# A fused S5 and LayerNorm kernel on one core: other queues for the early loads, other PSUM banks for the first transposes, a shorter TensorE warm-up and a new written order

## The chip, the core and the metric

The kernel runs on one core of a Trainium2 chip. The metric is device time in microseconds (us) of one execution. Matmuls run on TensorE (PE, with its weight loads in a row of their own, PEld), elementwise work on VectorE (DVE), ScalarE (ACT) and GpSimd (POOL); SyncE (SP), ACT and POOL issue DMAs from queues of their own. Every engine runs its own instructions strictly in the order in which they were written and waits for the others by semaphores.

## The reference

`x` is one sequence of 2048 tokens with 1024 features, in bf16, as all inputs are. The output is the sum of three terms:

```
xn  = layernorm(x)                                  # over the 1024 features
dt  = exp(log_dt);  L = exp(dt * (Lambda_re + i Lambda_im))
Bu  = xn @ (((L - 1) / Lambda)[:, None] * (B_re + i B_im)).T     # 1024 states, complex
h_t = L * h_{t-1} + Bu_t                            # a scan over the 2048 tokens
A   = 2 * real(h @ (C_re + i C_im).T) + xn * Dskip
r   = xn @ w_r;  the two tokens with the largest r are taken
y   = (silu(xn_sel @ w_gate) * (xn_sel @ w_up)) @ w_down * sigmoid(r_sel)
out = x + A + (xn, with y added to the rows of the two tokens)
```

## The kernel before

Tokens are worked on in 16 chunks of 128 (index c) and 8 frames of 256 (index f); the states in 8 blocks of 128 (index j). For a chunk: x is loaded (`x.c`, L164, L173 or L230); for chunks 0 to 5 DVE takes the statistics in two halves (`bs.c`, `bn.c`, L294 and L297), ACT makes 1/sqrt of the variance from a logarithm and an exponential (`rstd.c`, L262 and L263), DVE applies them (`applyA` and `apply.0` for the halves of chunk 0, L330; `apply.c`, L323), PE transposes the result into a PSUM bank by matmuls with the identity (`TpeA` and `Tpe.0`, L373; `Tpe.c`, L367), and ACT copies it to SBUF as `xnT` (`xnT.c`, L378 and L380; the second half of chunk 0 is copied by DVE, `xnT0`, L383). Chunks 6 to 15 are normalised by ACT and transposed by DMA.

For a frame and a block of states, PE multiplies `xnT` by the transposed B (`Bu.f.j`, L652, 16 matmuls; the first blocks are split by chunk into `Bh.f.j` and `Bu.f.j`), and ACT copies the result out (`u`, L658). For a chunk DVE multiplies by a table (L702, L703), runs the scans (L722), and multiplies back (`TO.c`, L763 to L765) into `hT`. PE then multiplies `hT` by C (`Y.c`, L839), DVE adds the skip term (L850), and the chunk is stored (L854). The carry from chunk to chunk is on POOL. The matmuls of the selected tokens are interleaved later.

The tables need the parameters Lambda_re, Lambda_im, log_dt and w_r. They are loaded as four pieces of 8 rows of one tile `prow` (L169), transposed by one PE instruction (`pP`, L467) and copied by DVE (`pcol`, L470). Then come a product (`angle`, L493 to L501), sines and cosines on ACT (`sin` L517, `first` L512 and L513, `cos` L520), an inverse by logarithm and exponential (`inv`, L530 and L531) and products on DVE (`rc`, L534, and others). ACT loads another function table before the sines (L505) and the first one again behind them (L508). POOL computes small factors (`kappa`, L565 to L571).

The order of all this is the string ORDER, written out by hand: `Plan.emit` calls the functions in exactly that order, and `Plan.run` only asserts that each one stands behind what it depends on and that buffers come free in time. The numbers for durations and keys in the `add` calls don't change the order. Outside ORDER, at the program's start, stand the loads of x.0, x.1, x.2 and of the parameters, ACT's first table load (L176), and the constants. PE starts with a warm-up (`warm.0` to `warm.22`): 23 steps, of which steps 8 to 10 are one matmul of 512 columns (`prime`, L282) and the others two matmuls of 128 columns (L399).

Of the kernel before, what the change touches and what calls it, by code (L numbers as in the profile page):

```python
# [25 lines left out]
B.0.0 xa x.0 x.1 B.0.1 bs.0 bn.0 nmean.0 start.0 x.3 x.2 rstd.0 bs.1 bn.1 applyA apply.0 bs.2 rstd.1 apply.1 nmr1.0 warm.0 warm.1 warm.2 warm.3 warm.4  # L26
warm.5 warm.6 warm.7 warm.8 warm.9 warm.10 warm.11 warm.12 B.1.1 warm.13 warm.14 warm.15 warm.16 warm.17 warm.18 warm.19 warm.20 warm.21 warm.22 TpeA
Tpe.0 xnT0 bn.2 bs.3 bn.3 xnT.0 pP.0 Tpe.1 xnT.1 Bh.0.0 Bu.0.0 B.1.0 B.3.0 nmean.1 nmr1.1 nmean.2 rstd.2 nmr1.2 apply.2 Tpe.2 nmr.2 rstd.3 nmean.3
pcol.0 rsum Bh.0.1 Bu.0.1 nmr.1 u.0.0 wr B.2.0 dt x.5 apply.3 Tpe.3 xnT.2 Bh.1.1 Bh.1.0 B.2.1 frq rad turns whole angle abs trig den x.4 xnT.3 Bu.1.0
Bu.1.1 B.3.1 u.0.1 sin bs.5 bn.5 first Bh.1.2 Bu.1.2 bs.4 x.6 B.4.1 cos u.1.0 u.1.1 Bu.1.3 log bn.4 nmr.3 nmr1.3 sq1.0 rstd.4 apply.4 inv.0 sq1.1 rc.0  # L30
R0.0 Bu.0.2 B.7.0 B.4.0 nmean.5 R.0 Tpe.4 u.1.2 Bu.0.3 rstd.5 apply.5 nmean.4 B.5.0 nmr.5 nmr1.5 u.1.3 Bu.0.4 inv.1 tan.0 u.0.2 Tpe.5 Bu.1.4 rc.1
tan.1 B.5.1 cs ntan.0 nmr1.4 kappa sum.6 R0.1 u.0.3 Bu.1.5 ts.0.0 ts.1.0 B.6.1 TI.0.0 nmean.6 R.1 E2c.0 x.7 u.0.4 B.6.0 B.7.1 C.0.0 cin.0.0 SC.0.0.0
ends xr.0 C.0.1 ntan.1 sq.6 u.1.4 x.8 Bu.0.5 Bu.0.6 u.1.5 xnT.4 u.0.5 Bu.0.7 Bu.1.6 sum.7 xnT.5 u.0.6 nmean.7 sq.7 Bu.1.7 nmr.0 ts.0.1 u.0.7 Bu.2.0
u.1.6 u.1.7 E2c.1 nmr.4 E2n.1 SC.0.0.1 cw.0.0 gb.0.0.0 cy.0.0 cin.1.0 gb.0.0.1 rstd.7 Bu.2.1 ts.1.1 E2s.1 TI.1.0 TI.0.4 TI.1.4 E2n.0 cin.0.4 C.1.0
SC.0.4.0 SC.0.4.1 u.2.0 u.2.1 nmr.7 E2s.0 apply.7 T.7 xr.1 Bu.2.2 Bu.2.3 Bu.2.4 u.2.2 Bu.2.5 gb.0.4.0 cw.0.4 gb.0.4.1 SC.1.0.0 cy.0.4 cin.1.4 nmr1.7
TO.0.0 u.2.3 cw.1.0 SC.1.0.1 cy.1.0 Drow rstd.6 nmr.6 apply.6 T.6 x.9 x.10 u.2.4 SC.1.4.0 cw.1.4 Bu.2.6 Bu.2.7 xnT.6 gb.1.0.1 seed.0.0 TO.0.4 seed.0.1
gb.1.0.0 Y.0.0 gb.1.4.0 u.2.5 u.2.6 SC.1.4.1 xs.0 xr.2 gb.1.4.1 xs.1 cin.2.0 cy.1.4 TI.2.0 TI.3.0 C.1.1 Y.0.1 Y.0.2 u.2.7 TO.1.0 sum.9 nmean.9
seed.1.0 xnT.7 Bu.3.0 Bu.3.1 u.3.0 Bu.3.2 sq.9 rstd.9 nmr1.9 nmr.9 TO.1.4 u.3.1 Y.1.0 Y.1.1 xm.0 cin.2.4 x.12 ADD.0.0 seed.1.1 out.0.0 apply.9 Y.0.3
SC.2.0.0 SC.2.0.1 Bu.3.3 cw.2.0 Bu.3.4 xm.1 T.9 u.3.2 Bu.3.5 ADD.1.0 cy.2.0 TI.4.0 gb.2.0.0 sum.8 out.1.0 ADD.0.1 gb.2.0.1 xs.2 nmean.8 cin.3.0 Y.1.2
Y.1.3 w.0 xm.2 sum.12 seed.2.0 nmean.12 xnT.9 SC.3.0.0 r.0 sq.8 rstd.8 nmr.8 cw.3.0 apply.8 x.11 u.3.3 u.3.4 u.3.5 SC.3.0.1 cy.3.0 cin.4.0 gb.3.0.1  # L40
TO.2.0 T.8 gb.3.0.0 ADD.1.1 out.1.1 SC.4.0.0 SC.4.0.1 out.0.1 cw.4.0 cy.4.0 cin.5.0 sq.12 Bu.3.6 Bu.3.7 rstd.12 xnT.8 Y.2.0 Bu.4.0 nmr.12 xr.3 nmr1.6
sum.11 seed.2.1 nmean.11 TO.3.0 Y.2.1 nmr1.12 ADD.2.0 u.3.6 seed.3.0 u.3.7 Y.2.2 Y.2.3 xs.3 xm.3 apply.12 Bu.4.1 gb.4.0.0 T.12 out.2.0 gb.4.0.1
seed.3.1 Y.3.0 TI.5.0 u.4.0 u.4.1 ADD.2.1 sum.10 SC.5.0.0 cw.5.0 xr.4 Bu.4.2 xs.4 Y.3.1 gb.5.0.0 u.4.2 sq.11 TO.4.0 SC.5.0.1 xr.5 Y.3.2 Y.3.3 seed.4.0
out.2.1 Bu.4.3 Bu.4.4 w.1 cy.5.0 w.2 nmean.10 sq.10 rstd.10 nmr.10 apply.10 T.10 gb.5.0.1 ADD.3.0 ADD.3.1 xnT.10 Y.4.0 Bu.4.5 rstd.11 u.4.3 Y.4.1
seed.4.1 w.3 xm.4 Bu.4.6 cin.6.0 TI.6.0 SC.6.0.0 SC.6.0.1 cw.6.0 nmr.11 ADD.4.0 apply.11 xr.6 Y.4.2 x.14 u.4.4 TO.5.0 u.4.5 gb.6.0.0 u.4.6 gb.6.0.1
nmr1.10 Bu.4.7 T.11 xnT.11 x.13 seed.5.0 seed.5.1 cy.6.0 out.3.1 TI.7.0 Y.4.3 ADD.4.1 w.4 Y.5.0 xs.5 Y.5.1 out.3.0 sum.13 u.4.7 Bu.5.0 Bu.5.1 out.4.0
xm.5 nmean.13 sq.13 xs.6 seed.6.0 cin.7.0 SC.7.0.0 SC.7.0.1 rstd.13 nmr.13 x.15 ADD.5.0 TO.6.0 gb.7.0.0 Y.5.2 Y.5.3 xr.7 Bu.5.2 gb.7.0.1 xm.6 apply.13
seed.6.1 u.5.0 Y.6.0 Y.6.1 sum.14 Bu.5.3 TI.8.0 ADD.5.1 nmean.14 sq.14 out.4.1 rstd.14 nmr.14 w.5 u.5.1 Bu.5.4 Y.6.2 out.5.0 cw.7.0 xr.9 cy.7.0
cin.8.0 SC.8.0.0 SC.8.0.1 TI.9.0 TO.7.0 u.5.2 Bu.5.5 xnT.12 cw.8.0 cy.8.0 cin.9.0 seed.7.0 Y.6.3 T.13 sum.15 xnT.13 nmean.15 sq.15 nmr1.11 ADD.6.0
ADD.6.1 rstd.15 nmr1.15 nmr.15 apply.15 T.15 u.5.3 Bu.5.6 gb.8.0.1 apply.14 xnT.15 gb.8.0.0 SC.9.0.0 SC.9.0.1 TO.8.0 cw.9.0 T.14 xnT.14 Y.7.0 out.5.1  # L50
u.5.4 Bu.5.7 u.5.5 r.1 xs.7 Y.7.1 seed.7.1 xr.8 u.5.6 u.5.7 nmr1.8 rsb seed.8.0 rT cand nmr1.14 Y.7.2 xm.7 ADD.7.0 Y.8.0 xs.8 xm.8 out.6.0 pI cy.9.0
cin.10.0 seed.8.1 idx gather gb.9.0.1 Bu.6.0 u.6.0 Bu.6.1 out.6.1 u.6.1 w.6 out.7.0 gb.9.0.0 TI.10.0 SC.10.0.0 SC.10.0.1 xs.9 TO.9.0 w.7 Bu.6.2 Bu.6.3
u.6.2 Y.8.1 Y.8.2 u.6.3 gb.10.0.0 bns gb.10.0.1 rstds Y.7.3 ADD.7.1 Bu.6.4 ADD.8.0 out.8.0 norm Y.8.3 ADD.8.1 hot Bu.6.5 cw.10.0 xm.9 out.8.1 seed.9.0
sT out.7.1 seed.9.1 xT cy.10.0 Bu.6.6 cin.11.0 mm.0 ymb0 u.6.4 u.6.5 Y.9.0 TI.11.0 Y.9.1 sig SC.11.0.0 SC.11.0.1 xr.10 u.6.6 seed.10.0 gb.11.0.0
ADD.9.0 Y.9.2 seed.10.1 gb.11.0.1 Bu.6.7 u.6.7 w.8 w.9 w.10 Y.9.3 TO.10.0 w.11 out.9.0 mm.1 TI.12.0 cw.11.0 xs.10 xm.10 cy.11.0 Y.10.0 Y.10.1 Y.10.2
exp.0 gu.0 ADD.9.1 ADD.10.0 xr.11 seed.11.0 guT.0 Bu.7.0 u.7.0 nmr1.13 cin.12.0 Y.10.3 w.12 w.13 w.14 w.15 xs.11 w.16 w.17 w.18 SC.12.0.0 gT.0
gb.12.0.0 cw.12.0 SC.12.0.1 sig1 mm.2 exp.1 gb.12.0.1 ADD.10.1 cy.12.0 xr.12 TO.11.0 Bu.7.1 w.19 w.20 w.21 w.22 w.23 Bu.7.2 seed.11.1 seed.12.0 u.7.1
u.7.2 Y.11.0 w.24 w.25 gu.1 guT.1 Y.11.1 xr.13 cin.13.0 out.9.1 Bu.7.3 u.7.3 mm.3 exp.2 TI.13.0 SC.13.0.0 SC.13.0.1 gb.13.0.0 gb.13.0.1 xm.11 ADD.11.0
seed.12.1 Bu.7.4 u.7.4 gT.1 out.10.1 xs.12 w.26 gu.2 Bu.7.5 u.7.5 Bu.7.6 u.7.6 TI.15.0 w.27 w.28 w.29 TO.12.0 Bu.7.7 u.7.7 guT.2 xm.12 gT.2 mm.4
Y.11.2 TO.13.0 out.10.0 w.30 Y.12.0 xs.13 exp.3 TI.15.4 TI.14.0 w.31 Y.12.1 Y.11.3 TI.15.6 ADD.11.1 w.32 w.33 mm.5 gu.3 cw.13.0 cy.13.0 out.11.0  # L60
seed.13.0 ADD.12.0 cin.14.0 SC.14.0.0 seed.13.1 gb.14.0.0 SC.14.0.1 xm.13 Y.12.2 Y.12.3 cw.14.0 cy.14.0 cin.15.0 Y.13.0 w.34 w.35 w.36 ADD.12.1 w.37
gb.14.0.1 w.38 w.39 xr.14 seed.14.0 w.40 w.41 out.11.1 TO.14.0 guT.3 Y.13.1 Y.13.2 Y.13.3 gT.3 ADD.13.0 seed.14.1 SC.15.4.0 SC.15.4.1 ADD.13.1 mm.6
mm.7 Y.14.0 SC.15.0.0 SC.15.0.1 xr.15 rows row_.3 row_.1 row_.2 Y.14.1 Y.14.2 Y.14.3 SC.15.6.0 SC.15.6.1 ymb hotY.14.1 hotY.14.0 xs.14 seed.15.0 xm.14
TO.15.0 ADD.14.0 seed.15.1 ADD.14.1 seed.15.2 out.12.1 TO.15.4 TO.15.6 out.12.0 hotY.15.0 Y.15.0 Y.15.1 Y.15.2 Y.15.3 Y.15.4 Y.15.5 Y.15.6 Y.15.7
hotY.15.2 hotY.15.1 Y.15.8 xs.15 xm.15 ADD.15.0 ADD.15.1 ADD.15.2 out.13.0 out.13.1 fix out.14.0 out.14.1 out.15.0 out.15.1 out.15.2
# [39 lines left out]
def kernel(  # L105
# [135 lines left out]

    add(("xa",), "none", 2.85, lambda: None, key=-1)
    for c in range(NCH):
        if c < 3:
            add(("x", c), "none", (3.35, 0.6, 0.6)[c], lambda: None, [("x", c - 1)] if c else [], key=c, takes=[("xt", c, [("apply", c)])])
        elif c == 3:
            add(("x", c), "SP", 0.45, lambda c=c: load_x(c), key=-89.85, takes=[("xt", c, [("apply", c)])], mb=0.28, lag=0.2)
# [917 lines left out]
```

## Time and profile before

| what | value |
|---|---|
| time, median of 3 runs | 255.83 us (255.74 to 256.82) |
| the profiled execution's own time | 255.56 us |
| its span | 253.8 us |
| PE busy | 246.7 us, 97% of the span, 2052 matmuls |
| DVE busy | 239.8 us, 94%, 312 instructions |
| ACT busy | 175.5 us, 69% |
| POOL busy | 93.1 us, 37% |
| DMA | 46.50 MB, mean 183 GB/s |
| chain that ended last | PE 65%, DVE 25%, POOL 3%, ACT 2%, DMA 1% |

The span runs from the first to the last instruction of the execution; about 1.8 us of the execution's time lie around it. Busy time of two engines overlaps. The chain is followed back from the last instruction to whatever released each step.

### The profile page before, as it was taken

Reading aid. Unit: us, or ns where it says so; the run is one execution under the profiler, and the core shown is the slowest. Engines: PE = TensorE matmul, PEld = TensorE weight load, DVE = VectorE, ACT = ScalarE, POOL = GpSimd, SP = SyncE. Lnnn points to the kernel's source line nnn. Section 1 sums busy time; section 2 is a strip of 40 time slices with the busy share of each in tenths; the row PEclk is TensorE's granted clock in tenths of the full one; section 3 lists DMA queues with packets and bytes.
Section 4 is the critical chain, followed back from the end, with each engine's and each line's share of the span. In section 5 each row is a group of like instructions: output and inputs, shape, how many; then the busy total and the mean of one; then the engine's idle time right before and its main releaser. Section 6 shows DMA issues by size and latency. Waiting matters only on the chain.

```text
span 253.8 us, 5220 instructions
## 1 busy us (share of the span) xinstructions
PE 246.7 (97%) x2052; PEld 167.0 (66%) x2052; DVE 239.8 (94%) x312; ACT 175.5 (69%) x302; POOL 93.1 (37%) x130
## 2 busy tenths in 40 slices
...
GB/s 196 225 228 184 191 254 274 148 134 198 99 159 45 83 89 242 40 256 228 120 89 1 105 166 69 76 3 155 321 340 381 361 316 388 384 250 357 23 68 83
DMA packets 66277, 46.50 MB, mean 183 GB/s; under 512 B 45828, under 2 KB 52362, under 8 KB 66252
## 3 DMA queue, kind: packets, MB, share of 16 engines
...
q8 instruction: 16, 0.26, 0.4%
q0 software_dynamic: 112, 0.27, 0.3%
...
## 4 chain that ended last, share of the span: by engine, by line
PE 65%; DVE 25%; POOL 3%; ACT 2%; DMA 1%; issue 1%; ACTq 0%; DVEq 0%; POOLq 0%
PE pY L839 38%; PE pB L652 22%; DVE gf L722 7%; PE pG L1043 3%; DVE v L703 3%; DVE m L702 2%; DVE m L764 1%; DVE hT L763 1%; DVE ot L850 1%; DVE hT L765 1%; PE pD L1083 1%; DMA xt<-in_A_x_dram 1%; DVE st L294 1%; DVE ts L585 1%; DVE E2c L591 1%
## 5 line engine op out<-in xcount | busy, mean ns | idle before, releaser
L652 PE MATMUL pB<-xnT,BT 128*128 128x256 bf16 (+1 forms) x1104 | 116.9, 265 | 0.6 <-ACT xnT L378 0.3
L839 PE MATMUL pY<-CT,hT 128*128 128x512 bf16 (+1 forms) x528 | 115.7, 373 | 0.2 <-DVE hT L765 0.2
L652 PEld LDWEIGHTS <-BT 128*128 128x128 bf16 x1104 | 100.9, 98 | 16.4 <-issue 1.7
L839 PEld LDWEIGHTS <-hT 128*128 128x128 bf16 x528 | 50.8, 98 | 55.4 <-issue 2.1
L738 POOL TENSOR_TENSOR cw<-gf,tL 128x16 f32<-128x16 f32 (+1 forms) x34 | 41.1, 1210 | 110.8 <-DVE gf L722 101.3
L722 DVE TENSOR_TENSOR_SCAN gf<-R,v 128x1040 f32<-128x1040 f32 (+1 forms) x34 | 68.8, 2056 | 0.5
L658 ACT CAST u<-pB 128x512 bf16<-128x512 f32 x64 | 35.7, 577 | 18.3 <-PE pB L652 15.5
L815 ACT ACTIVATE pY<-xr,nmr_all,rstd_all 128x512 f32<-128x512 bf16 (+1 forms) x33 | 24.9, 763 | 29.2 <-DVE ot L850 24.7
L728 ACT CAST gb<-gf 128x1024 bf16<-128x1024 f32 (+1 forms) x34 | 31.4, 941 | 8.0 <-DVE gf L722 8.0
L850 DVE TENSOR_TENSOR ot<-pY,ot 128x512 bf16<-128x512 f32 (+1 forms) x33 | 21.5, 663 | 3.3 <-PE pY L839 2.1
L765 DVE TENSOR_TENSOR hT<-hT,m 128x2048 bf16<-128x2048 bf16 (+2 forms) x20 | 20.2, 1012 | 0.7
L703 DVE TENSOR_TENSOR v<-u,m 128x2048 bf16<-128x2048 bf16 (+2 forms) x20 | 20.2, 1012 | 0.7
L702 DVE TENSOR_TENSOR m<-u,E1t 128x2048 bf16<-128x2048 bf16 (+2 forms) x20 | 20.1, 1005 | 0.6
L764 DVE TENSOR_TENSOR m<-gb,E2s 128x2048 bf16<-128x2048 bf16 (+2 forms) x20 | 20.3, 1014 | 0.0
L824 ACT ACTIVATE ot<-xr,nmr_all,rstd_all 128x1024 bf16<-128x1024 bf16 x16 | 19.8, 1237 | 0.6 <-DMA out_dram<-ot 0.5
L763 DVE TENSOR_TENSOR hT<-gb,E2c 128x2048 bf16<-128x2048 bf16 (+2 forms) x20 | 20.0, 1000 | 0.0
L753 POOL CAST v<-cy 128x16 bf16<-128x16 f32 (+1 forms) x17 | 12.7, 747 | 1.0
L754 POOL TENSOR_TENSOR v<-cy,v 128x16 bf16<-128x16 f32 (+1 forms) x17 | 12.5, 738 | 1.4
L334 ACT ACTIVATE xn<-xt,nmr_all,rstd_all 128x1024 bf16<-128x1024 bf16 x10 | 12.4, 1237 | 0.2
L309 ACT ACTIVATE xn<-xt,nmean_all 128x1024 bf16<-128x1024 bf16 x10 | 11.5, 1150 | 0.2
L829 DVE TENSOR_TENSOR ot<-ot,Drow 128x1024 bf16<-128x1024 bf16 x16 | 10.9, 680 | 0.0
L303 ACT ACTIVATE xn<-xt 128x1024 bf16<-128x1024 bf16 x10 | 10.5, 1050 | 0.0
...
## 6 DMA issues: line engine op xcount, KB each, us to landing
...
```

Of the source, the lines that this page charges most:

```text
L652: nc.tensor.matmul(out=pB[:, ri, ts_], lhsT=BT[ri][j][:, k, :], rhs=xnT_frame(f)[:, k, ts_], start=(k == 0), stop=(k == DT - 1))
L658: nc.scalar.copy(out=u_tiles[f][:, :, j, :], in_=pB_tiles.pop((f, j))[:])
L702: nc.vector.tensor_tensor(out=m[:, :, js, :], in0=u[:, ::-1], in1=E1t[:, :, js, :], op=ALU.mult)
L703: nc.vector.tensor_add(out=rot, in0=u, in1=m[:, :, js, :])
L722: nc.vector.tensor_tensor_scan(out=flat(gf), data0=flat(R[:, js, :]), data1=flat(v[:, ri, js, :]), initial=0.0, op0=ALU.mult, op1=ALU.add)
L728: nc.scalar.copy(out=gb_tiles[c][:, ri, js, :], in_=gf_tiles[c, js.start, ri][:, :, 2:])
L738: nc.gpsimd.tensor_tensor(out=cw_tiles[c, js.start][:, ri, :, 0:n], in0=g.unsqueeze(1).to_broadcast([128, 2, n]), in1=tL[:, ri, :, js], op ...
L764: nc.vector.tensor_tensor(out=m[:, :, js, :], in0=g[:, ::-1], in1=both(E2s, js), op=ALU.mult)
L765: nc.vector.tensor_add(out=rot, in0=rot, in1=m[:, :, js, :])
L815: nc.scalar.activation(out=pY[:, 0:d_.stop - d_.start], in_=y_tiles["xr", c][:, d_], func=ACT.Identity, bias=nmr_all[:, c:c + 1], scale=rs ...
L839: nc.tensor.matmul(out=pY, lhsT=h_tiles[c][:, ri, j, :], rhs=CT[ri][h][:, j, d0:d0 + w], start=False, stop=end, skip_group_check=True)
L850: nc.vector.tensor_add(out=ot, in0=y_tiles.pop(("pY", c, dh))[:, 0:d_.stop - d_.start], in1=ot)
```

## The change

1. ACT's queue issues four transfers before its table load in place of six: Lambda_re, Lambda_im, log_dt and x.1. The fourth parameter, w_r, is issued by POOL behind its two iotas, and x.2 by SP.
2. SP issues x.3 and x.2 directly behind x.0, and only then the first transposing loads of B (`B.0.0`, `B.0.1`); `x.3` was behind these two.
3. Chunk 0 is transposed into two PSUM banks, one half into the bank with the tag T and the other into that with the tag misc; before, both halves were in T. Chunk 1 uses one of the three banks of the tag B; before, misc.
4. The warm-up has 15 steps in place of 23, that is 16 matmuls of 128 columns fewer.
5. ORDER is rewritten from end to end. On PE, `pP` now stands ahead of chunk 0's transposes, and both `Tpe.3` and `Tpe.2` stand ahead of `Bh.0.1`.

```diff
 ORDER = """
-B.0.0 xa x.0 x.1 B.0.1 bs.0 bn.0 nmean.0 start.0 x.3 x.2 rstd.0 bs.1 bn.1 applyA apply.0 bs.2 rstd.1 apply.1 ...
+x.3 xa bs.0 x.2 warm.0 ... x.0 bn.0 x.1 warm.10 warm.11 bs.1 bn.1 rstd.0 applyA ... pP.0 apply.0 bs.3 pcol.0 apply.1 TpeA Tpe.0 ...
...
-    load_param(nc.scalar, 0)
-    for c in (1, 2):
-        nc.scalar.dma_start(out=xt_tiles[c][:], in_=x2[c * T:(c + 1) * T, :])
-    for i in range(1, 4):
+    for i in range(3):
         load_param(nc.scalar, i)
+    nc.scalar.dma_start(out=xt_tiles[1][:], in_=x2[T:2 * T, :])
     nc.scalar.preload_act_table_set("natural_log_exp_and_others")
...
     nc.vector.tensor_copy(out=tt[:], in_=t_i[:])
+    load_param(nc.gpsimd, 3)
...
-        pT_tiles[c] = psum.tile([128, DT, 128], BF16, name="pT", tag="misc" if odd else "T")
+        pT_tiles[c] = psum.tile([128, DT, 128], BF16, name="pT", tag="B" if c == 1 else "misc" if odd else "T", bufs=3 if c == 1 else 1)
...
     def transpose_half(h):
-        if h == 0:
-            pT_tiles[0] = psum.tile([128, DT, 128], BF16, name="pT", tag="T")
+        pT_tiles[0, h] = psum.tile([128, DT // 2, 128], BF16, name="pT", tag="misc" if h else "T")
...
-    NWARM = 23
+    NWARM = 15
```

The first place is the start of ACT's instructions, up to the first logarithm of `rstd.0`. Before:

```order
L169 DMA prow<-in_A_Lambda_re_dram 8x128
L173 DMA xt<-in_A_x_dram 128x1024 x2
L169 DMA prow<-in_A_Lambda_im_dram 8x128
L169 DMA prow<-in_A_log_dt_dram 8x128
L169 DMA prow<-in_B_w_r_dram 8x128
L176 ACT_TABLE_LOAD
L262 ACTIVATE lv<-mv,eps_t 128x1
```

The same place now:

```order
L169 DMA prow<-in_A_Lambda_re_dram 8x128
L169 DMA prow<-in_A_Lambda_im_dram 8x128
L169 DMA prow<-in_A_log_dt_dram 8x128
L173 DMA xt<-in_A_x_dram 128x1024
L174 ACT_TABLE_LOAD
L261 ACTIVATE lv<-mv,eps_t 128x1
```

The transfer of w_r and that of x.2 are gone from ACT, and x.1 stands behind three parameters in place of one.

The second place is DVE from `applyA` and `apply.0` (the row with x2) on; mv holds a chunk's mean and variance, st its partial statistics. Before:

```order
L330 TENSOR_SCALAR xn<-xt,mv,rstd_all 128x512 x2
L294 BN_STATS st<-xt 128x6
L323 TENSOR_SCALAR xn<-xt,mv,rstd_all 128x1024
L383 COPY xnT<-pT 128x4x128
L294 BN_STATS st<-xt 128x6
L297 BN_AGGR mv<-st 128x2
L294 BN_STATS st<-xt 128x6 x2
L297 BN_AGGR mv<-st 128x2
L323 TENSOR_SCALAR xn<-xt,mv,rstd_all 128x1024
L470 CAST pcol<-pP 128x32
```

The same place now:

```order
L329 TENSOR_SCALAR xn<-xt,mv,rstd_all 128x512 x2
L293 BN_STATS st<-xt 128x6
L468 CAST pcol<-pP 128x32
L322 TENSOR_SCALAR xn<-xt,mv,rstd_all 128x1024
L381 COPY xnT<-pT 128x4x128
L293 BN_STATS st<-xt 128x6
L296 BN_AGGR mv<-st 128x2
L293 BN_STATS st<-xt 128x6 x2
L296 BN_AGGR mv<-st 128x2
L471 CAST wr_cm<-pcol 128x8
L477 TENSOR_TENSOR scr<-scr,pcol 128x8
L478 SCALAR_TENSOR_TENSOR frq<-scr,pcol 128x8
```

The copy of the parameters moves ahead of `apply.1`, and the applies of chunks 3 and 2 come behind the parameters' products.

The third place is ACT around the sines and cosines (sf and cf hold them, th the angle, gf the inverse). Before:

```order
L517 ACTIVATE sf<-th 128x1024
L512 ACTIVATE scr<-th 128x8
L513 ACTIVATE scr<-cf,halfpi 128x8
L520 ACTIVATE cf<-cf,halfpi 128x1024
L658 CAST u<-pB 128x2x256 x2
L508 ACT_TABLE_LOAD
L262 ACTIVATE lv<-mv,eps_t 128x1
L263 ACTIVATE rstd_all<-lv 128x1
L530 ACTIVATE gf<-th 128x4x128
```

The same place now:

```order
L510 ACTIVATE scr<-th 128x8
L511 ACTIVATE scr<-cf,halfpi 128x8
L518 ACTIVATE cf<-cf,halfpi 128x1024
L656 CAST u<-pB 128x2x256
L515 ACTIVATE sf<-th 128x1024
L506 ACT_TABLE_LOAD
L656 CAST u<-pB 128x2x256
L261 ACTIVATE lv<-mv,eps_t 128x1
L262 ACTIVATE rstd_all<-lv 128x1
L528 ACTIVATE gf<-th 128x4x128
```

The sine moves from ahead of the cosine to behind it, and one of the two copies of `u` to behind the table load.

## Rows read from the trace of the kernel before

**Rows 1.** Stretches: us, busy us (count) by engine, clock, DMA share, GB/s.

```profile
1.36:3.04 1.68, 1.68 (x16) 1.68 (x17) 0.96 (x6) 0.00 (x0) 0.61 (x5) 1.00 0.47 139
3.04:4.32 1.28, 1.28 (x5) 0.46 (x4) 0.89 (x2) 0.00 (x0) 0.00 (x0) 1.00 0.98 349
4.32:5.07 0.75, 0.75 (x9) 0.75 (x7) 0.72 (x3) 0.21 (x1) 0.12 (x1) 1.00 1.15 296
5.07:6.02 0.95, 0.95 (x19) 0.94 (x17) 0.94 (x2) 0.95 (x1) 0.13 (x1) 1.00 1.30 279
14.23:78.07 63.84, 63.84 (x579) 51.47 (x576) 61.43 (x90) 56.48 (x106) 27.48 (x46) 1.00 0.88 184
...
83.26:249.40 166.14, 166.14 (x1264) 101.54 (x1265) 160.51 (x183) 106.70 (x175) 56.44 (x60) 1.00 0.58 189
```

**Rows 2.** Chain that ended last, near the middle: start us, us, what.

```profile
81.97 1.24 DVE hT L765
...
83.26 1.90 PE pY L839 x8
```

**Rows 3.** Chain that ended last among the first 12 us.

```profile
1.36 3.17 DMA xt<-in_A_x_dram
...
4.55 0.28 ACTq L169
...
4.86 1.28 ACT L176
...
6.48 0.21 ACT rstd_all L263
```

**Rows 4.** DVE in order of time: start us, us, what [idle before <-releaser].

```profile
4.78 1.23 DVE L294 BATCH_NORM_STATS2 st<-xt 128x6 f32<-128x512 bf16 x2
...
6.71 0.74 DVE L330 TENSOR_SCALAR xn<-xt,mv,rstd_all 128x512 bf16<-128x512 bf16 x2 [0.46 <-ACT rstd_all L263]
...
15.88 0.69 DVE L501 TENSOR_SCALAR cf<-th 128x1024 int32<-128x1024 int32 x1
...
21.40 0.55 DVE L323 TENSOR_SCALAR xn<-xt,mv,rstd_all 128x1024 bf16<-128x1024 bf16 x1 [0.56 <-ACT rstd_all L263]
...
29.48 1.31 DVE L585 TENSOR_TENSOR ts<-sf,scr 128x512 f32<-128x512 f32 x2 [0.46 <-POOL scr L571]
```

**Rows 5.** ACT in order of time.

```profile
2.23 0.36 ACTq L169 DMA_DIRECT2D prow<-in_A_Lambda_im_dram  x1
...
8.87 0.58 ACT L378 COPY xnT<-pT 128x512 bf16<-128x512 bf16 x1 [1.76 <-DVE xnT L383]
...
16.01 1.07 ACT L517 ACTIVATE sf<-th 128x1024 f32<-128x1024 f32 x1
...
22.46 0.57 ACT L658 CAST u<-pB 128x512 bf16<-128x512 f32 x1
```

**Rows 6.** The tiles of x, first 16 us: SP's issues (ns), landing.

```profile
L230 SPq DMA_DIRECT2D xt<-in_A_x_dram x4: 507/519/584, 5.2 to 15.7; - x4
...
DMA to landing us min/median/max: 2.1/3.1/3.5
```

**Rows 7.** SP in order of time.

```profile
3.05 2.10 SPq L234 DMA_TRANSPOSE BT<-in_A_B_im_dram  x1
```

**Rows 8.** The tiles of B, first 16 us.

```profile
DMA to landing us min/median/max: 3.7/3.8/4.0
```

**Rows 9.** PE in order of time.

```profile
4.32 1.86 PE L399 MATMUL warm<-ident 128*128 128x128 bf16 x24
7.19 0.72 PE L373 MATMUL pT<-ident,xn 128*128 128x128 bf16 x8 [1.00 <-DVE xn L330]
...
8.56 0.62 PE L367 MATMUL pT<-ident,xn 128*128 128x128 bf16 x8 [0.54 <-DVE xn L323]
9.50 1.97 PE L652 MATMUL pB<-xnT,BT 128*128 128x128 bf16 x32 [0.33 <-ACT xnT L378]
```

**Rows 10.** The transfer that POOL issues for the selected tokens.

```profile
DMA to landing us min/median/max: 3.5/3.5/3.5
```

More of the change, by code (lines that the diff above doesn't have):

```diff
@@ L25 @@
 ORDER = """
[L26 to L65, printed above, removed]
+x.3 xa bs.0 x.2 warm.0 warm.1 warm.2 warm.3 warm.4 warm.5 warm.6 warm.7 start.0 warm.8 warm.9 x.0 bn.0 x.1 warm.10 warm.11 bs.1 bn.1 rstd.0 applyA
@@ new lines @@
+rstd.1 nmean.0 nmr.0 warm.12 warm.13 warm.14 pP.0 apply.0 bs.3 pcol.0 apply.1 TpeA Tpe.0 nmr1.0 Tpe.1 xnT.0 nmean.1 B.0.0 B.0.1 xnT0 Bh.0.0 xnT.1
+Bu.0.0 dt bn.3 nmr.1 B.1.0 bs.2 bn.2 rstd.3 rstd.2 wr frq apply.3 Tpe.3 apply.2 Tpe.2 rad B.1.1 Bh.0.1 B.2.0 Bu.0.1 trig nmean.2 xnT.2 Bh.1.0 B.2.1
+xnT.3 Bu.1.0 rsum u.0.0 turns whole x.5 x.4 angle abs bs.5 bn.5 Bh.1.1 Bu.1.1 bs.4 nmr1.1 bn.4 u.0.1 first cos u.1.0 B.4.0 sin Bh.1.2 Bu.1.2 sq1.0
+sq1.1 den log u.1.1 rstd.4 inv.0 u.1.2 inv.1 Bu.0.2 B.3.0 apply.4 B.3.1 Bu.0.3 Tpe.4 B.4.1 Bu.0.4 rc.0 R0.0 R.0 tan.0 u.0.2 rc.1 x.6 B.5.0 B.5.1
```

63 lines of the change are left out of this document (49 added, 14 removed).

## The prediction

> **What bounds the kernel now.** I read the stretches first [rows 1]. From 83.26 us to 249.40 us PE is busy for all of the 166.14 us, and from 14.23 to 78.07 for all of the 63.84. DVE beside it has little left: 160.51 of 166.14. So the body is full of matmuls that the change doesn't remove. The chain of waits comes next: at 83.26 it passes from DVE's last product for chunk 2 (`TO.2`, 1.24 us from 81.97) to PE's first matmuls of `Y.2` [rows 2]. In front of that point there are places where PE waits; behind it there is none until the tail. Whatever the change gains must therefore move the instant 83.26. If the end of DVE's `TO.2` and PE's own work before it both come x earlier, the end comes x earlier; if only one does, nothing moves, since before they meet within a few tenths of a us there.
>
> The start is read last, because all of DVE's work hangs on one instruction: `applyA`, at a = 6.71, after 0.46 us of idle time in which DVE waits for the rstd of chunk 0 [rows 4]. ACT could not make it, since its sixth DMA issue waited until x.1 had landed (issued 1.36, 3.17 us on its way), then took 0.28, and only then came the table load of 1.28, and the logarithm and exponential, done at 6.69 [rows 3]. The 6.71 is thus ACT's and not DVE's.
>
> **The queue on ACT.** With four issues there is no wait for a landing. The fourth issue of before started at 2.23 [rows 5]; in its place now stands x.1, behind three parameters of about 0.36 each, so I put it at 2.1. The table load runs from about 2.5 to 3.8, and rstd.0 is there at about 5.4, 1.3 earlier. Not all of that reaches `applyA`: DVE's order still has both halves of chunk 1's statistics and their sum in front of it. They start at 4.78 and DVE is free at 6.71 - 0.46 = 6.25 [rows 4], so 1.5 us. Hence the new `applyA` is a' = (landing of x.1) + 1.5, and x.1 is now issued 0.75 later than before. Without the other edits this part gives at most 0.46.
>
> When does x.1 land? Shortest way: 2.1 + 2.1 = 4.2; middle: 2.1 + 3.1 = 5.2; longest: 2.1 + 3.5 = 5.6 [rows 6]. A second bound is by bytes. The DMA engines are loaded to 0.98 and above from 3.04 on [rows 1]. By 3.04 some 139 GB/s x 1.68 us = 0.23 MB have come, by 4.32 another 349 x 1.28 = 0.45. Ahead of x.1 or beside it now stand x.0 and x.3, and x.2, each 0.26 MB. Three tiles (0.79 MB) are in at 4.32 + 0.11/0.296 = 4.7, four (1.05 MB) at 5.6. I take 5.0, inside both, so a' = 6.5, which is 0.2 before the old 6.71; bounds 4.6 and 5.5, a' = 6.1 to 7.0.
>
> **SP's queue.** x.3 and x.2 come ahead of B.0.0 and B.0.1: two issues of 0.52 [rows 6] push the second from 3.05 [rows 7] to about 4.15. Its landing, 3.8 to 4.0 later [rows 8], comes at 8.15. PE needs it for `Bh.0.0` at a' + 2.5 = 9.0, so 0.85 us of cover hides it. That cover also holds if SP's issue drags as that of 3.05 did (2.10 long, some 0.7 over an ordinary one). Cost 0, at worst some 0.2.
>
> **The two banks.** Before, ACT's copy of chunk 0's first half stood 1.76 us behind DVE's copy of the other half of the same PSUM tile [rows 5], and `Bh.0.0` waited 0.33 for it [rows 9]. In two tiles they run side by side. That gives `Bh.0.0` about 0.3 us: it was at a + 2.79, it comes at a' + 2.5. Chunk 1's transposes in a B bank hold that bank until ACT has copied them; four PSUM tiles later it is used again, long after. Cost 0.
>
> **The order on PE.** `Bu.0.0` then waits about 0.3 for chunk 1's copy, and `Tpe.3` about 0.8 for `apply.3`, which on DVE now stands behind the statistics of chunks 3 and 2 and the parameters' products; before, there was no such wait. The first waits of before (1.00, 0.54, 0.33 [rows 9]) are replaced by these. By my walk PE is through the same set of tasks at a' + 8.25 against a + 7.52, so 0.5 late at 14.8 for a' = 6.5. But between 78.07 and 83.26 it waited 0.4 to 0.6 for DVE, so this lateness ends in waits that exist today: PE reaches `Y.2.0` at about 82.9, as before.
>
> **DVE and ACT between `applyA` and the tables.** DVE does the same instructions from `applyA` to the absolute value of the angle (15.88 + 0.69 = 16.57, a + 9.86 [rows 4]), so that ends at a' + 9.86. Here ACT's order costs: the sine (1.07 [rows 5]) stood ahead of the cosine and ran while DVE still worked on the absolute value, half of it for nothing; now it stands behind, with one `u` of 0.57 [rows 5] moved past the table load. I get the inverse 0.58 later relative to `applyA`, and DVE waits for it (it waited 0.56 for rstd.4 at 21.40 already [rows 4], and this wait grows). Against that, DVE's wait of 0.46 at 29.48 for POOL's small factors [rows 4] goes: their inputs come as early as before and the products of chunks 0 to 3 on POOL no longer stand in front of them. Sum: +0.58 - 0.46 = +0.12, bounds -0.46 (the wait goes, and no new one comes) and +0.6 (only the new one).
>
> **The warm-up.** 16 matmuls in 1.68 us are 105 ns each, and 19 in the stretch from 5.07 on are 50 ns each [rows 1]: at the first pace 128 columns are at 1.2 GHz, at the second at 2.4, though the granted clock reads 1.00 in all of these rows. The rise came at about 5.1. The 15 steps end after 8 of the 24 matmuls that start at 4.32 [rows 9], at 4.32 + 8 x 0.105 = 5.16, just behind the rise. Then PE idles until `TpeA` at a' + 0.48 = 7.0, some 1.8 us where before it was 1.0 [rows 9]. I take no cost, since the pace held over the idle 1.0; that it holds over 1.8 no row shows. Upper bound below.
>
> **The parameter on POOL.** It is issued at about 1.6. POOL's one comparable transfer took 3.5 us to land [rows 10], so 5.1; the lower bound by x's rows is 1.6 + 2.1 = 3.7. PE's parameter transpose now stands in front of `TpeA`, and DVE's copy of it in front of `apply.1` at a' + 1.35 = 7.85. Landing by about 7.7 costs nothing: 2.6 us of cover. The Trainium skill's page "SBUF — State Buffer", section "SBUF: two separate sides", speaks against this edit: a DMA issued from GpSimd has its descriptors written by GpSimd's cores, which VectorE locks out of a shared port during some of its instructions; it gives 620 ns alone and some 3100 ns behind one. By that rule, 2.5 us later, an estimate from that page, the landing is 7.6, at the very edge, and the sum would still be the same; no run here has such a transfer near VectorE's copies.
>
> **Sum.** `applyA` -0.2, DVE's order +0.12, warm-up, banks, SP and parameter 0: -0.1 us at `TO.2`, thus at 83.26 and at the end. PE's order would allow -0.1 too. Against the profiled execution's own 255.56 us (span 253.8 and 1.8 around it) that is 255.5; against the median of 255.83, which is 0.27 above it, 255.7. I say 255.6.
>
> **Rivals.** *The start's gain goes through.* If x.1 lands at 4.6 and POOL's wait goes while the sine costs nothing, DVE gains 0.6 + 0.46, together 1.1: 254.5; with all of the 1.3 that ACT gains, 254.3. For it: PE's gain in `Bh.0.0` and its waits would allow it. Against it: x.1 goes later into loaded DMA engines. *The clock falls in the idle 1.8 us* and PE does the first transposes and products at 105 ns. As at the beginning, it would need some 3.7 us (1.36 to 5.1) to come back, in which 1.85 us of work is lost, up to 2.4 for the 48 matmuls to the end of `Bh.0.0`. Waits of 0.54 and 0.33 [rows 9] and the later ones cover 0.9 to 1.1, so about +1.3: 256.9, and 257.1 by the median. It decides once `TpeA`'s matmuls start 105 ns apart. For it: the idle time nearly doubles. Against: PE was fast for less than a us before both idles, and before it held. *The parameter is late:* beyond 7.7 everything on DVE and PE shifts one to one; a landing at 9.0 gives +1.3. Against: 2.6 us of cover. *Nothing is gained:* x.1 lands at 5.5 or later, a' = 7.0, and the time is +0.3 to +0.5: 256.1.
>
> **Chances.** Forecast 0.50; nothing gained 0.10; the gain goes through 0.22; clock 0.10; parameter 0.08. About 0.5% (1.3 us, so 254.55 and 257.1) is what a measurement of this kernel can tell from no change. Below 254.55 lies most of the gain's case, 0.18. Above 257.1 lie two thirds of the clock's and the parameter's, with some for a wait I have not seen: 0.14. Within: 0.68. The likeliest case has 255.1 to 256.2 of its own; the range of 254.2 to 257.3 takes in the gain's 254.3 and the clock's 257.1.
>
> **What would show it.** In the profile after: the table load starts by 2.6 without a wait; x.1 lands near 5.0 and `applyA` starts 1.5 later; ACT's first copy no longer waits for DVE's; PE waits before `Tpe.3`; ACT's inverse later than `applyA` + 15.3; no wait for POOL's factors; `Y.2.0` at about 83.2 with DVE as its releaser; then PE full to the tail. The forecast is wrong if PE's first matmuls of `Tpe` start 105 ns apart, if `applyA` comes before 6.1, or if PE waits anywhere behind `Y.2.0`, since the later order is rewritten too and I found no wait in it.

## The result and the profile after

The changed kernel is slower: 257.69 us (257.12 to 258.30, 7 runs) against 256.11 us (255.74 to 256.82, 7 runs) for the kernel before on the same chip, a ratio of 1.0066 with a 95% interval of 1.0043 to 1.0089. The forecast was 255.6, and its range ended at 257.3. The profiled execution took 258.08 us (span 256.3) against 255.56.

The chain that ended last is the first thing to read. Before, 65% of the span on it were PE's and 25% DVE's. In the changed kernel's page:

```profile
PE 89%; DMA 6%; DVE 2%; SPq 1%; issue 1%; ACTq 0%
```

DVE is nearly off the chain and a DMA is on it. Its first pieces, in the same view as [rows 3] (start us, us, what), tell which:

```profile
2.02 5.27 DMA xt<-in_A_x_dram
...
7.31 1.30 DVE st L293 x2
...
8.63 0.21 DVE mv L296
...
10.65 1.03 PE pT L366 x8
11.68 3.03 PE pB L650 x32
```

x.1, issued at 2.02, is on its way for 5.27 us where it was 3.17 [rows 3]; the statistics of chunk 1 wait for it. ACT, in order of time, has long been ready (answers to [rows 5] and to the table load in [rows 3]):

```profile
2.02 0.39 ACTq L173 DMA_DIRECT2D xt<-in_A_x_dram  x1
2.44 1.28 ACT L174 ACT_TABLE_LOAD   x1 [2.44 <-issue]
...
5.00 0.20 ACT L262 ACTIVATE rstd_all<-lv 128x1 f32<-128x1 f32 x1
...
9.82 0.58 ACT L376 COPY xnT<-pT 128x512 bf16<-128x512 bf16 x1 [0.42 <-PE pT L371]
```

The table load starts at 2.44 and rstd.0 is there at 5.20. It waits until DVE, in order, reaches `applyA` (answers to [rows 4]; idle time and its releaser in brackets):

```profile
7.31 1.29 DVE L293 BATCH_NORM_STATS2 st<-xt 128x6 f32<-128x512 bf16 x2 [2.68 <-DMA xt<-in_A_x_dram]
8.63 0.21 DVE L296 BATCH_NORM_AGGREGATE mv<-st 128x2 f32<-128x12 f32 x1
8.76 0.68 DVE L329 TENSOR_SCALAR xn<-xt,mv,rstd_all 128x512 bf16<-128x512 bf16 x2
...
17.80 0.69 DVE L499 TENSOR_SCALAR cf<-th 128x1024 int32<-128x1024 int32 x1
...
25.00 0.69 DVE L532 TENSOR_TENSOR gf<-gf,cf 128x512 f32<-128x512 f32 x1 [0.64 <-ACT gf L529]
```

So `applyA` starts at 8.76, 2.05 us later than before. PE's rows answer to [rows 9]:

```profile
4.33 1.06 PE L397 MATMUL warm<-ident 128*128 128x128 bf16 x8
5.32 0.20 PE L465 MATMUL pP<-ident,prow 32*128 32x32 bf16 x1
9.18 1.03 PE L371 MATMUL pT<-ident,xn 128*128 128x128 bf16 x8 [3.65 <-DVE xn L329]
10.65 1.03 PE L366 MATMUL pT<-ident,xn 128*128 128x128 bf16 x8 [0.44 <-DVE xn L322]
11.47 3.24 PE L650 MATMUL pB<-xnT,BT 128*128 128x128 bf16 x32
14.55 1.06 PE L366 MATMUL pT<-ident,xn 128*128 128x128 bf16 x16
15.45 6.75 PE L650 MATMUL pB<-xnT,BT 128*128 128x128 bf16 x118
```

Eight transposes of 128 columns take 1.03 us here and took 0.62 to 0.72 before [rows 9], and the 32 products of the first block take 3.24 us and took 1.97 [rows 9]. PE runs at the lower of its two paces, 1.2 GHz in place of 2.4, until about 14.5. The granted clock in this profile's stretches still reads 1.00 there, so the pace has to be read from counts; three of the seven executions of the changed kernel have a mean granted clock of 0.987, and further down there are profiles whose granted clock shows the fall.

From 15.45 on nothing is lost. The stretches of the changed kernel at the slow pace and from there to the tail, and the one of before that holds the same matmuls (at 14.23 it has done 32 products of 1.79 us more than the changed kernel at 15.45, so it begins at 12.44), in the view of [rows 1]. After:

```profile
9.18:15.45 6.27, 5.83 (x65) 5.57 (x66) 6.17 (x18) 4.11 (x10) 2.40 (x8) 1.00 0.96 212
15.45:252.00 236.55, 235.14 (x1921) 158.85 (x1938) 227.85 (x278) 169.31 (x288) 78.00 (x109) 1.00 0.67 183
```

Before:

```profile
12.44:249.40 236.96, 236.48 (x1939) 158.70 (x1937) 228.82 (x280) 170.15 (x289) 88.99 (x109) 1.00 0.66 184
```

PE enters this work 3.01 us late. DVE's last additions start at 251.98, and at 249.44 before, so 0.47 is given back and the end is 2.54 late. The loss lies wholly in the first 15 us.

### The profile page after: what moved, and what is told of

Same layout as the page of the kernel before. It is cut to its first block, busy times and chain, and to the rows that moved or that the text cites. A ratio compares the mean times of both kernels' runs of the same rounds, so it can differ in the third digit from the quotient of the medians.

```text
span 256.3 us, 5170 instructions
## 1 busy us (share of the span) xinstructions
PE 246.2 (96%) x2017; PEld 168.1 (66%) x2036; DVE 239.9 (94%) x312; ACT 175.5 (68%) x302; POOL 83.4 (33%) x131
## 4 chain that ended last, share of the span: by engine, by line
PE 89%; DMA 6%; DVE 2%; SPq 1%; issue 1%; ACTq 0%
PE pB L650 44%; PE pY L837 39%; DMA wt<-in_B_w_down_dram 4%; PE pG L1041 3%; DMA xt<-in_A_x_dram 2%; PE pT L366 1%; SPq L1029 1%; PE r_ps L392 1%; DVE st L293 1%; DVE ot L848 1%; ACTq L169 0%; PE pD L1081 0%; PE pY L842 0%; PE pR L906 0%; PE pU L1061 0%
## 5 line engine op out<-in xcount | busy, mean ns | idle before, releaser
L650 PE MATMUL pB<-xnT,BT 128*128 128x256 bf16 (+1 forms) x1104 | 118.2, 267 | 0.0
L837 PE MATMUL pY<-CT,hT 128*128 128x512 bf16 (+1 forms) x509 | 113.6, 372 | 1.3 <-issue 0.5
L650 PEld LDWEIGHTS <-BT 128*128 128x128 bf16 x1104 | 102.4, 99 | 15.8 <-issue 0.4
L736 POOL TENSOR_TENSOR cw<-gf,tL 128x16 f32<-128x16 f32 (+1 forms) x34 | 39.2, 1153 | 119.1 <-DVE gf L720 110.6
L752 POOL TENSOR_TENSOR v<-cy,v 128x16 bf16<-128x16 f32 (+1 forms) x17 | 10.4, 612 | 1.4
L293 DVE BATCH_NORM_STATS2 st<-xt 128x6 f32<-128x512 bf16 x12 | 7.8, 677 | 3.1 <-DMA xt<-in_A_x_dram 3.1
```

The lines of the kernel that those rows point to most:

```text
L650: nc.tensor.matmul(out=pB[:, ri, ts_], lhsT=BT[ri][j][:, k, :], rhs=xnT_frame(f)[:, k, ts_], start=(k == 0), stop=(k == DT - 1))
L736: nc.gpsimd.tensor_tensor(out=cw_tiles[c, js.start][:, ri, :, 0:n], in0=g.unsqueeze(1).to_broadcast([128, 2, n]), in1=tL[:, ri, :, js], op ...
L837: nc.tensor.matmul(out=pY, lhsT=h_tiles[c][:, ri, j, :], rhs=CT[ri][h][:, j, d0:d0 + w], start=False, stop=end, skip_group_check=True)
```

## The experiments

All ratios are to the kernel before on the same chip, with the 95% interval; the changed kernel itself has 1.0066. First, what made x.1 late. Three edits, each alone.

**x.1 first on ACT's queue.**

```diff
+    nc.scalar.dma_start(out=xt_tiles[1][:], in_=x2[T:2 * T, :])
     for i in range(3):
         load_param(nc.scalar, i)
-    nc.scalar.dma_start(out=xt_tiles[1][:], in_=x2[T:2 * T, :])
```

> The changed kernel with x.1 issued first on ACT's queue, ahead of the three parameters. Theory Q (x.1 came late because it stood behind three transfers on its queue and was issued 0.7 us later than before): x.1 lands at 4.5 to 5.2, applyA starts at 6.0 to 6.7 in place of 8.76, the clock holds over the shorter idle time, and the time falls by 2.5 to 4 us, to 254 to 255.2. Theory X (it came late because x.3 and x.2 now stand in front of the other loads on SP and share the DMA engines): x.1 still lands after 6 us, and the time stays within 1 us of the changed kernel's 257.7. Theory W (POOL's transfer of w_r disturbs it): also no gain.

Measured: 1.0002 (0.9983 to 1.0022), 255.86 against 255.62 us. DVE no longer waits for x.1 at all: its statistics start at 5.10, directly behind chunk 0's, and `applyA` at 6.50. That is theory Q's place of `applyA`, but not its time: PE's pace still falls, and the granted clock shows it here. Stretches (us, PE busy with count, granted clock, DMA share, GB/s):

```profile
7.00:8.00 1.00, 0.63 (x8) 0.75 1.25 241
8.00:9.00 1.00, 0.62 (x7) 0.50 1.28 282
9.00:10.00 1.00, 1.00 (x12) 0.50 0.82 174
...
14.00:15.00 1.00, 1.00 (x18) 0.83 1.12 315
15.00:16.00 1.00, 1.00 (x22) 1.00 1.08 324
```

PE had been idle from 4.8 to 6.9 but for one small transpose. The clock is at half from about 7.5 to 14.3, for 5 us of which PE is busy without a gap. The profiled execution is one of the longer ones (256.82, mean granted clock 0.987); three of the ten have a mean of 0.999 and took 255.11 to 255.40. So in some executions this edit seems to keep the clock as well, and the run does not separate the two gains.

**x.2 behind B.0.1 on SP.**

```diff
-x.3 xa bs.0 x.2 warm.0 ...
+x.3 xa bs.0 warm.0 ...
-... nmean.1 B.0.0 B.0.1 xnT0 ...
+... nmean.1 B.0.0 B.0.1 x.2 xnT0 ...
```

> The changed kernel with x.2 issued by SP behind B.0.0 and B.0.1, not ahead of them. Theory X: one tile of 0.26 MB fewer beside x.1, which then lands at about 5.0, and applyA starts at 6.5; the time falls by 2 to 3.5 us. Theory Q and theory W: x.1 still lands after 6.5 us, the time is that of the changed kernel within 0.7 us.

Measured: 1.0029 (1.0014 to 1.0043), 256.38 us. x.1 is there at 5.47 in place of 7.31 and `applyA` starts at 6.92; the clock is at 0.50 from 8 to 14 us. Theory X also holds a part. The place of x.3, which stands in front as well, was not varied.

**w_r on ACT behind x.1, nothing on POOL.**

```diff
     nc.scalar.dma_start(out=xt_tiles[1][:], in_=x2[T:2 * T, :])
+    load_param(nc.scalar, 3)
...
-    load_param(nc.gpsimd, 3)
```

> The changed kernel with w_r as a fifth transfer on ACT's queue, behind x.1, and none on POOL. Theory W: x.1 lands at about 5.0, applyA at 6.5, and the time falls by 2 us or more. Theories Q and X: x.1 lands after 6.5 as in the changed kernel, and the time is the same within 0.7 us; the table load starts 0.3 us later, which nothing waits for.

Measured: 1.0066 (1.0046 to 1.0085), 257.57 us, as the changed kernel. DVE's wait for x.1 ends at 6.42 in this profile, and theory W falls. The landing moves from one execution to the next: in the three profiles with exactly the changed kernel's order of transfers it was 6.3, 7.2 and 7.3, and some of the spread of the times between executions may come from there.

Second, the clock. **A warm-up of 50 steps, so that PE never idles before `TpeA`.**

```diff
-    NWARM = 15
+    NWARM = 50
```

> The changed kernel with a warm-up of 50 steps, so that PE works until about 9.1 us, whenever x.1 lands. Theory C (the idle 3.65 us before the first transposes cost PE its clock): the transposes of chunk 0 still start at about 9.2, but their matmuls start 56 ns apart and not 107, PE has done Bu.0.0 some 1.5 to 2.4 us earlier, and the time falls by as much, to 255.3 to 256.2. If PE's pace there is hidden by waits for DVE and ACT, the time stays within 0.4 of 257.7.

Measured: 1.0042 (1.0026 to 1.0057), 256.69 us. The clock reads 1.00 in all of the first 17 us, and with x.1 there at 6.33 PE's first 16 products take their full pace:

```profile
4.25 4.52 PE L397 MATMUL warm<-ident 128*128 128x128 bf16 x78
...
10.12 1.06 PE L650 MATMUL pB<-xnT,BT 128*128 128x128 bf16 x16
11.39 1.05 PE L650 MATMUL pB<-xnT,BT 128*128 128x128 bf16 x16 [0.21 <-ACT xnT L378]
```

It regains 0.24% of 255.6, 0.6 us, and not the 1.5 to 2.4 expected; as the two intervals overlap, the 0.6 rests on the profiles too, which give the same (0.62, below). Much of the slow pace then lies in time in which PE would have waited for DVE and ACT: with the clock held it waits 0.23, 0.21 and 0.43 us for them up to `Bh.0.1`, and in the changed kernel, behind its first transposes, only 0.44.

**The warm-up of 23 steps in the changed kernel, x.1 still late.**

```diff
-    NWARM = 15
+    NWARM = 23
```

> The changed kernel with the 23 steps of before and its late x.1. In this kernel applyA starts at 7.8 to 8.8, so after 23 steps (6.0 us) PE still idles for 2.3 to 3.2 us. If the clock falls after some 2 us of idle time, as in the two kernels with 15 steps, it falls here too: matmuls 107 ns apart, time within 0.5 us of the changed kernel, 1.2 to 1.7 us over the kernel before. If 23 steps are enough for themselves, the time is that of the warm-up of 50 steps, about 1.0 us over before.

Measured: 1.0066 (1.0039 to 1.0093), 257.74 us. x.1 was there at 7.18, PE idled 2.83 us behind the 23 steps, and the granted clock is 0.50 from 9 to 15. With x.1 late, the old warm-up is too short as well.

**The kernel before with 15 steps and nothing else.**

```diff
-    NWARM = 23
+    NWARM = 15
```

> The kernel before with a warm-up of 15 steps in place of 23 and nothing else. Theory C (15 steps are too few, since PE then idles for about 2 us before TpeA at 7.2): the granted clock falls to 0.50 at 8 to 9 us as it did with x.1 first, the matmuls of Bh.0.0 start 107 ns apart, and the time rises by 0.5 to 1.5 us. Rival: the clock falls only after more than the 2 us of idle time that stand here; the time is the same within 0.3 us.

Measured: 1.0045 (1.0017 to 1.0072), 257.35 us against 255.56. This edit alone costs 0.4 to 1.8 us. The interval is wide because the executions differ: two of the twelve took 255.83 and 255.90 at a mean granted clock of 0.998, near the 255.56 of the kernel before, and eight took 257.31 to 257.86. The profiled one took 256.28. PE's rows show an idle time of 2.01 where it was 1.00 [rows 9], and the stretches where the clock falls, with x.1 on time:

```profile
7.09 0.72 PE L373 MATMUL pT<-ident,xn 128*128 128x128 bf16 x8 [2.01 <-DVE xn L330]
...
8.46 1.03 PE L367 MATMUL pT<-ident,xn 128*128 128x128 bf16 x8 [0.54 <-DVE xn L323]
```

```profile
7.00:8.00 1.00, 0.84 (x9) 1.00 0.90 292
8.00:9.00 1.00, 0.54 (x6) 0.52 0.98 223
9.00:10.00 1.00, 1.00 (x12) 0.50 1.11 190
...
11.00:12.00 1.00, 1.00 (x17) 0.78 1.07 217
12.00:13.00 1.00, 1.00 (x22) 1.00 1.12 157
```

The first eight transposes behind the idle time still run at the full pace (0.72 us, as in [rows 9]); the fall comes a us later. The first matmuls behind a gap don't tell whether the clock falls, and the prediction's sign for this rival, first transposes 105 ns apart, would have missed it here.

Third, the other parts. **w_r by POOL in the kernel before.**

```diff
-    for i in range(1, 4):
+    for i in range(1, 3):
         load_param(nc.scalar, i)
...
+    load_param(nc.gpsimd, 3)
```

> The kernel before with w_r issued by POOL and five transfers on ACT. Theory Q2 (ACT's wait for x.1 ahead of its sixth issue is what set applyA before): the table load starts by 3.0 without a wait, rstd.0 is there by 5.5, applyA starts when DVE has chunk 1's statistics, at 6.2 to 6.3 in place of 6.71, and as DVE sets the end the time falls by 0.3 to 0.5 us. Rival (w_r by POOL comes late, or its gain is eaten elsewhere): no change within 0.2 us or slower.

Measured: 0.9977 (0.9951 to 1.0003), 255.17 us. The table load starts at 2.96, and `applyA` at 5.95, 0.76 us earlier than before. The profiled execution, one of the longer ones (256.20), spends that again, mostly on waits for loads (PE's waits):

```profile
PE pD L1084 <- DMA wt<-in_B_w_down_dram: 1.2, 2, 0.9
PE pT L368 <- DVE xn L324: 0.5, 1, 0.5
PE pB L653 <- DMA BT<-in_A_B_re_dram: 0.5, 1, 0.5
```

The median moved as expected, but the interval reaches to no change: inconclusive by a little.

**The two banks in the kernel before.**

```diff
-            pT_tiles[0] = psum.tile([128, DT, 128], BF16, name="pT", tag="T")
+        pT_tiles[0, h] = psum.tile([128, DT // 2, 128], BF16, name="pT", tag="misc" if h else "T")
...
-        pT_tiles[c] = psum.tile([128, DT, 128], BF16, name="pT", tag="misc" if odd else "T")
+        pT_tiles[c] = psum.tile([128, DT, 128], BF16, name="pT", tag="B" if c == 1 else "misc" if odd else "T", bufs=3 if c == 1 else 1)
```

> The kernel before with chunk 0's transposes in two banks and chunk 1's in a B bank, and nothing else. The forecast's reading: ACT's copy of the first half no longer waits 1.76 us for DVE's copy, Bh.0.0 starts about 0.3 us earlier, and as DVE sets the end the time is the same within 0.3 us. Rival: PE sets the end, and the time falls by 0.3 us.

Measured: 0.9992 (0.9967 to 1.0017), 255.71 us. ACT's copy waits 0.39 us for PE and no longer 1.76 for DVE; `Bh.0.0` starts at 8.95 in place of 9.50; the time is the same. What PE gained there it waits for DVE later (0.5 us at `hT`, 0.2 before).

Last, versions with both repairs. **x.1 first, 31 steps.**

```diff
+    nc.scalar.dma_start(out=xt_tiles[1][:], in_=x2[T:2 * T, :])
     for i in range(3):
         load_param(nc.scalar, i)
-    nc.scalar.dma_start(out=xt_tiles[1][:], in_=x2[T:2 * T, :])
...
-    NWARM = 15
+    NWARM = 31
```

> The changed kernel with x.1 first on ACT's queue and a warm-up of 31 steps, which ends at about 6.9 us. If the late x.1 and the clock are all that the change lost, the granted clock stays 1.00, applyA starts at 6.5, Bh.0.1 at about 12.6 where it started at 14.3 with 15 steps, and the time is 0.2 to 0.7 us under that of the kernel before. If the later order costs something of its own (theory O), the time is not below the kernel before.

Measured: 0.9977 (0.9955 to 1.0000), 255.23 us. The clock holds, `applyA` starts at 6.69, and `Bh.0.1` at 12.76. The median is below that of the kernel before, but the interval just reaches no change; that theory O falls is shown by the next version, which has the same later order.

**x.1 second, 23 steps.**

```diff
-    for i in range(3):
+    load_param(nc.scalar, 0)
+    nc.scalar.dma_start(out=xt_tiles[1][:], in_=x2[T:2 * T, :])
+    for i in range(1, 3):
         load_param(nc.scalar, i)
-    nc.scalar.dma_start(out=xt_tiles[1][:], in_=x2[T:2 * T, :])
...
-    NWARM = 15
+    NWARM = 23
```

> The changed kernel with x.1 second on ACT's queue, behind Lambda_re as in the kernel before, and the 23 steps of before. If x.1's place on the queue is what made it late (theory Q), it lands at 4.4 to 4.9 and applyA starts at 5.9 to 6.4, with the clock held; the time is 0.6 to 1.2 us under the kernel before. If x.3 and x.2 on SP make x.1 late by themselves (theory X), it lands after 5.3, applyA starts after 6.8, and the time is not below the kernel before.

Measured: 0.9962 (0.9944 to 0.9980), 254.80 us against 255.74. This beats both kernels. PE's rows:

```profile
7.22 0.72 PE L372 MATMUL pT<-ident,xn 128*128 128x128 bf16 x8 [1.15 <-DVE xn L330]
8.69 0.62 PE L367 MATMUL pT<-ident,xn 128*128 128x128 bf16 x8 [0.75 <-DVE xn L323]
9.15 1.06 PE L651 MATMUL pB<-xnT,BT 128*128 128x128 bf16 x16
```

x.1 was there before DVE wanted it (5.41), as chunk 0's second half came only at 4.55; `applyA` started at 6.80. So in this execution `applyA` is no earlier than in the kernel before, 6.71, and neither theory's account fits it: `applyA` is where theory X has it, and the time is in theory Q's range. But the profiled execution took 255.34, only 0.22 less than that of the kernel before. Whether `applyA` comes earlier in the executions near the median of 254.80 no profile shows; chunk 0's second half, which it waits for here, came at 3.71 in the last version's profile below.

**The same with x.2 behind B.0.1.**

```diff
-x.3 xa bs.0 x.2 warm.0 ...
+x.3 xa bs.0 warm.0 ...
-... nmean.1 B.0.0 B.0.1 xnT0 ...
+... nmean.1 B.0.0 B.0.1 x.2 xnT0 ...
```

> The kernel with x.1 second and 23 steps, and x.2 issued by SP behind B.0.1. Theory X: x.1 lands another 0.3 to 0.8 us earlier and the time falls by as much as applyA moves. Theory Q: no difference; or a loss, if x.2 now comes too late for its statistics or B.1.0 for PE.

Measured: 0.9965 (0.9946 to 0.9985), 255.05 us, `applyA` at 6.70: no difference. Once x.1 stands second, x.2's place is indifferent.

**The same with `applyA` and `apply.0` between the halves of chunk 1's statistics.**

```diff
-... bs.1 bn.1 rstd.0 applyA
+... bs.1 rstd.0 applyA apply.0 bn.1
-... warm.22 pP.0 apply.0 bs.3 ...
+... warm.22 pP.0 bs.3 ...
```

> The kernel with x.1 second and 23 steps, and on DVE applyA and apply.0 ahead of the second half of chunk 1's statistics. If DVE's work alone sets the end, its order within these 2 us changes nothing: same within 0.2 us. If PE's first transposes do, they start 0.6 us earlier and the time falls by up to 0.5 us; if DVE idles before applyA for the rstd, the time rises by that idle time.

Measured: 0.9965 (0.9939 to 0.9990), 255.13 us. `applyA` starts at 5.25 and PE's first transposes at 5.91, but PE's next transposes (`Tpe.1`) wait 1.50 for `apply.1`, and the time is the same.

## Why the prediction was wrong

*The landing of x.1: wrong, and the largest part.* The sum has -0.2 at `applyA`, and +2.05 was measured. The step "a' = landing + 1.5" held (7.31 + 1.45 = 8.76). The landing did not: forecast 5.0 within 4.6 to 5.5, measured 7.3 in this profile and 6.3 to 7.3 over the three with this order of transfers. Both bounds took rates of the kernel before as given: the longest landing of x, 3.5 us [rows 6], and 296 to 349 GB/s [rows 1]. The DMA queues show what came in their place. From 3.5 to 4.0 us, before and after (queue and kind: packets, MB, share of 16 engines; q10 holds ACT's transfers, q1 SP's, q0 POOL's). Before:

```profile
q10 hardware_dynamic: 98, 0.18, 95.2%
q1 hardware_dynamic: 2, 0.00, 0.2%
```

After:

```profile
q10 hardware_dynamic: 11, 0.02, 71.5%
q1 hardware_dynamic: 35, 0.05, 32.3%
q0 software_dynamic: 29, 0.00, 3.9%
```

Eleven packets of x.1 took 71.5% of 16 engines for 0.5 us, 0.52 us each; before it was 0.08. In the stretch from 3.5 to 4.5 the DMA engines are busy and move 123 GB/s. This comes with the order of transfers and not with one execution: from 3.0 to 4.5 us the core moved 198 to 227 GB/s in the four profiles in which x.1 stands behind three parameters and x.2 in front of B's loads (208 in this one), and 289 to 383 in all others (350 before). It is not always x.1's packets that are slow: with 50 steps those of SP took 0.25 us each from 3.0 to 3.5. What of x.1 is left by 6.0 stands beside B's transposing loads. After, from 6.0 to 6.5:

```profile
q1 hardware_dynamic: 175, 0.07, 171.6%
q10 hardware_dynamic: 14, 0.02, 12.8%
```

The runs show what moves the landing: x.1's place behind the parameters (first: there by 5.1) and x.2 in front on SP (moved: 5.47), but not POOL's transfer. Moving x.1 alone took the ratio from 1.0066 to 1.0002, 1.6 us, with some of the clock's cost in it. With the 0.6 of the longer warm-up that makes 2.2; x.1 first and 31 steps together gave 2.3 (1.0066 to 0.9977). Why the transfers are so slow in this order is not settled.

*The warm-up's cost of 0: wrong.* I took it from an idle time of 1.0 us and noted that 1.8 has no row. At 2.0 us the clock falls in the profile of the kernel before with 15 steps alone. The rival had this mechanism at +1.3 us with a chance of 0.10; alone it measured 1.2 us by the ratio, within 0.4 to 1.8. In the changed kernel it costs 0.6, since it lies beside waits. I also treated it as independent of x.1: a later x.1 lengthens the idle time, so the two go together, and 23 steps don't hold either.

*"DVE sets the end at 83.26": wrong for the changed order.* Behind its first transposes PE waits for nothing that matters in the changed kernel (the chain is 89% PE). Its largest waits (engine and line, what was waited for: us in total, times, longest):

```profile
PE pT L371 <- DVE xn L329: 3.7, 1, 3.7
PE warm L397 <- POOL ident masks.py:199: 1.4, 1, 1.4
PE pY L837 <- issue: 0.5, 3, 0.2
PE pT L366 <- DVE xn L322: 0.4, 1, 0.4
```

The two waits of before near 83.26 are gone:

```profile
79.37 3.65 PE L652 MATMUL pB<-xnT,BT 128*128 128x256 bf16 x32 [0.24 <-ACT u L658]
...
83.26 1.90 PE L839 MATMUL pY<-CT,hT 128*128 128x512 bf16 x8 [0.23 <-DVE hT L765]
```

Together they are 0.47 us, just what is given back. The prediction read them as 0.4 to 0.6 of waiting for DVE; half of it was for ACT. That the rewritten order removes them is inferred from these rows; no run changes the later order alone. In the profile of the version with x.1 second the stretch from `Bh.0.1` (12.88) to DVE's last additions (249.24) is 0.64 shorter than in the kernel before (12.44 to 249.44), and as `Bh.0.1` comes 0.44 later there, 0.20 is left. Where the rest of the 0.9 us between the medians lies no profile shows. I had walked the order only as far as `Y.2.0` with DVE's work of before.

Where the profiled execution's 3.01 us at `Bh.0.1` came from, counted from `applyA`: `applyA` 2.05. From `applyA` to `Bh.0.1` it is 15.45 - 8.76 = 6.69, with the clock held 13.85 - 7.78 = 6.07 (50 steps), before 12.44 - 6.71 = 5.73. So the clock is 0.62, and the remaining 0.34 I put down to the order of statistics and applies on DVE, which no run isolates. With the 0.47 given back, 2.05 + 0.62 + 0.34 - 0.47 is the 2.54 at the end.

*Right:* the table load without a wait (2.44; 2.5 forecast) and rstd.0 (5.20; 5.4). ACT's copy beside DVE's. B.0.1 in time in spite of an issue of 3.14 us. `Tpe.3`'s wait, 0.43 with the clock held, where I had 0.8. From `applyA` to the absolute value 17.80 + 0.69 - 8.76 = 9.73 (9.86). The inverse later against `applyA`: 16.24 against 15.87, so +0.37 where I had +0.58. POOL's wait of 0.46 gone. w_r came 3.0 us after its issue by POOL, at 4.6, and PE's parameter transpose ran at 5.32 without a wait; in the nine other profiles in which POOL issues it, it took 3.3 to 4.2 us, and with x.1 first the transpose waited 0.54 for it. By the lockout of which the Trainium skill's page "SBUF — State Buffer" tells, in "SBUF: two separate sides", the prediction estimated 7.6 for the landing; it came well before that in all of these profiles, and whether a shorter lockout is part of the 3.0 to 4.2 us no run here shows.
